# An attention kernel with a long convolution beside it: engines held to the source's order, and another order of the convolutions

## The chip, the cores and the metric

One core of a Trainium2 chip. The metric is the time of the program on the device in microseconds, the median of several runs. The engines are TensorE (PE; its weight loads are PEld), VectorE (DVE), ScalarE (ACT), GpSimd (POOL) and SyncE (SP). Here POOL and SP do hardly more than start DMAs.

## What is computed

Two independent blocks over 2048 positions; their results stand side by side in the output.

```python
# A: attention, 32 heads of 16, one shared k and v
q = (x @ wq) in 32 heads;  k = x @ wk;  v = x @ wv
p = softmax(q k^T / 4);    a = concat_heads(p v) @ wo
# B: 512 channels
k_shift = short causal convolution of k, 4 taps per channel
kv = k_shift * v
y  = long causal convolution of kv with ssm_k (2048 taps, by FFT) + kv * ssm_D
b  = q * y
```

## The kernel before

**Attention.** A *step* is one tile of 128 keys for four heads and 512 queries: `scores` (L655, PE) fills two score tiles for step i + 2, two exponentials (L663, ACT) turn them into `p`, and `pv` (L672, PE) adds `p` times v to the accumulator `acc`. There are 512 steps; 16 of them, a *group*, finish one accumulator, which VectorE copies out (`ao`, L682). The loop is `attend`. After each step it calls `fill.step(i)`.

**Fill.** `_Fill` holds five generators ("threads"). Each yields what its next piece costs in nanoseconds of PE and of DVE, or that it wants to wait some steps. At each step both accounts get a rate; a thread may go on while its accounts are positive, the first in the list first, and at most one piece with PE work per step. `RATES` lists (from step, PE rate, DVE rate); `Q_AT` lists the steps from which the four quarters of the queries are projected. The threads:

- `rest_of_q`: queries `q = x wq` (L186 with `xT,wq`), cut to two f16 parts (L525 to L530) and written to DRAM (`qd`), from where `stack` loads them (`st`, at the fifth step of a group, for the next group); and a bound (L539 to L548).
- `conv_pe`: the TensorE side of B, in two halves of 256 channels (`blk`). `long_load` and `long_forward` transform the filter `ssm_k` (`hin`; transposes L243, copies L245, products with the table `ff`, copies L193) into a spectrum `ch`. `short_load` and `short_forward` load windows of k (`kk`) and v, do the short convolution and the product with v on VectorE (L295 to L303) and transform the result `a` into a spectrum `cx`. `backward` transforms the product back (`sp,fi`) and multiplies by q (L364).
- `conv_dve`: the VectorE side: 16-point transforms (`dft16`: L124 to L137, L169 to L175) of both spectra, their product (L330), the transform back.
- `wo_heads` and `wo_part`: for each two accumulators, load the sums and the values back from DRAM (`rl`, `o`), invert the sums (L716, L717), spread them through DRAM (`rd`, `r`), scale (L724), then the products with `wo` (L186 with `wo,o`), added into `wp` (L758, L760).

Two PSUM banks have the tag `f`: one holds `acc`, the other the product of the fill, until VectorE has copied it.

**Order.** A scheduler sets the order of the instructions of ACT, DVE, POOL and SP after the source has been recorded; inside `manual_schedule(engines={PE})` PE alone keeps the order in which the source wrote its instructions. In the kernel before, that block takes in the prologue (load x, transposes, k, v, the first queries) and the attention.

Of the kernel before, what the change touches and what calls it, by code (L numbers as in the profile page):

```python
# [37 lines left out]
FT = 4  # L38
PB = 5

RATES = [(0, 440.0, 1650.0), (470, 920.0, 1650.0)]

Q_AT = 0, 50, 160, 290


def _tables():
# [29 lines left out]
WAIT = -1.0  # L76
# [3 lines left out]
class _Emit:  # L80
# [289 lines left out]
    def conv_pe(self):  # L370

        yield from self.conv_load()
        self.sp = {}
        hin = self.long_load(0)
        ch = self.spectrum()
        yield WAIT, 4
        for blk in range(D // CB):
            yield from self.long_forward(blk, hin, ch)
            self.sp["ch", blk] = ch
            self.seen.add(("ch", blk))  # L380
            tpb, kk = self.short_load(blk)
            if blk:
                yield from self.after(("y", blk - 1))
                yield from self.backward(blk - 1, *self.sp["y", blk - 1])
            cx = self.spectrum()
            yield from self.short_forward(blk, tpb, kk, cx)
            self.sp["cx", blk] = cx
            self.seen.add(("cx", blk))
            if blk == 0:
                hin = self.long_load(1)  # L390
                yield from self.after(("p", 0))
                ch = self.spectrum()
        yield from self.after(("y", 1))
        yield from self.backward(1, *self.sp["y", 1])

    def conv_dve(self):
        nat = [0, 1, 2, 3]
        for blk in range(D // CB):
            yield from self.after(("ch", blk))
            ch = self.sp["ch", blk]  # L400
            yield from self.dft16(ch, nat, nat, -1)
            yield from self.after(("cx", blk))
            cx = self.sp["cx", blk]
            yield from self.dft16(cx, nat, nat, -1)
            f1, f2 = self.places
            yield from self.product(cx, ch)
            self.seen.add(("p", blk))
            yield from self.dft16(cx, f2, f1, 1)
            self.sp["y", blk] = cx, self.places
            self.seen.add(("y", blk))  # L410
# [193 lines left out]
    def rest_of_q(self):  # L604
        for c, first in enumerate(Q_AT):
            while self.step < first:
                yield WAIT, 1
            for g in range(4):
                if c == 0 and g < 2:
                    continue  # L610
                b = None
                for dk in range(4):
                    yield (920, 0, HOLD) if dk < 3 else (920, 2600)
                    b = b or self.bank()
                    self.q_mm(g, c, b, dk)
                self.q_out(g, c, b)
                yield WAIT, 2
                yield 350, 1100
                self.bound(g, c, self.bank())
            self.seen.add(f"q{c}")  # L620
            if c < 2:
                self.xT[c + 2] = self.w.tile([P, 4, 512], F32, tag="xt", bufs=2, name=f"xT{c + 2}")
                self.nc.sync.dma_start(self.xT[c + 2], self.xd[c])
        self.flag()
# [364 lines left out]
def body(ctx, tc, I, out, parts="ab"):  # L989
    fpool = ctx.enter_context(tc.tile_pool(name="fl", bufs=1))  # L990
    ok = fpool.tile([1, 1], I32, name="ok")
    with ExitStack() as st:
        em = _Emit(st, tc, I, out)
        em.ok = ok
        st.enter_context(tc.manual_schedule(engines={mybir.EngineType.PE}))
        em.prologue()
        threads = [em.rest_of_q(), em.conv_pe(), em.wo_part(), em.wo_heads(), em.conv_dve()]
        em.attend(_Fill(threads, RATES))
    if "a" in parts:
        rv = tc.nc.values_load(ok[0:1, 0:1], min_val=0, max_val=1)  # L1000
        with tc.If(rv < 1):
            _general(tc, I, out)
# [21 lines left out]
```

## Time and profile before

| | us |
|---|---|
| median of 3 runs (1159.46 to 1162.69) | 1161.17 |
| the profiled execution | 1153.92 |
| its span, first to last instruction | 1152.1 |
| PE busy | 1059.8 |
| ACT busy | 989.6 |
| DVE busy | 633.8 |
| POOL busy | 87.8 |

The profiled execution took 1.8 us more than its span, and 0.6% less than the median of the runs. Busy time is the union of an engine's instructions; a busy PE is not PE at its peak, since ends of matmuls are modelled. The mean granted TensorE clock was 0.989. In rows of groups, the columns behind the count are the busy time, the mean length of one in ns, and the idle time just ahead of them with what ended it. Lines are those of the kernel before; in the changed kernel those of `load` (L413) and all behind it stand four lower.

### The profile page before, as it was taken

The numbers are of one execution on the slowest core, as the hardware profiler recorded it, in microseconds if no ns is written. First come the engines' busy times: TensorE is split into PE (matmuls) and PEld (weight loads), VectorE is DVE, ScalarE is ACT, GpSimd is POOL, SyncE is SP. The second block draws the span as 40 slices with busy tenths as digits, with TensorE's granted clock in tenths as the row PEclk, the third lists the DMA queues.
The fourth block names the chain that finished last, engine by engine and source line by source line (L and its number), as shares of the span: only waits on it lengthen the run. The fifth ranks groups of instructions, "written<-read, shape, count | busy, mean of one in ns | idle before, by whom it ended". The sixth has DMA issues, their size and how long they took to land.

```text
span 1152.1 us, 21936 instructions
## 1 busy us (share of the span) xinstructions
PE 1059.8 (92%) x8975; PEld 260.8 (23%) x8975; DVE 633.8 (55%) x914; ACT 989.6 (86%) x1041; POOL 87.8 (8%) x140
## 2 busy tenths in 40 slices
PE   6699999999899988999999899998999899999996
PEld 3222221221222111122222222221222111122321
DVE  3422221279976999951226932228738999711143
ACT  2399998999799878899999799999799899899882
POOL 1000000031110000000012100022110000000300
PEclk9899999999999999999999999999999999999999
DMA  8412111263241010121114211226221211121311
GB/s 283 159 33 75 59 36 54 80 187 101 67 145 57 28 45 26 56 86 34 35 59 154 81 42 34 64 92 190 95 72 54 85 43 45 44 73 29 129 33 44
DMA packets 49094, 89.55 MB, mean 78 GB/s; under 512 B 11308, under 2 KB 26202, under 8 KB 47964
## 3 DMA queue, kind: packets, MB, share of 16 engines
q1 hardware_dynamic: 36108, 46.42, 12.4%
q0 software_dynamic: 11648, 40.89, 11.1%
q8 instruction: 72, 1.18, 0.4%
q10 hardware_dynamic: 1232, 0.78, 0.2%
q14 instruction: 34, 0.28, 0.1%
HBM read 63.04 MB, written 25.02 MB: 76 GB/s over the span
## 4 chain that ended last, share of the span: by engine, by line
PE 52%; DVE 30%; ACT 6%; issue 6%; DMA 5%; SPq 0%; POOL 0%; ACTq 0%; DVEq 0%
PE f L672 24%; PE s L655 13%; PE f L186 13%; DVE sp L124 9%; ACT p L663 6%; DVE sp L330 3%; DVE a L301 2%; DVE t L299 2%; DVE t L330 1%; DMA o<-od 1%; DMA hin<-in_B_ssm_k 1%; DVE sp L175 1%; DVE u L173 1%; DVE sp L174 1%; DMA xb<-in_A_x 1%
## 5 line engine op out<-in xcount | busy, mean ns | idle before, releaser
L663 ACT ACTIVATE p<-s 128x1024 f32<-128x1024 f32 x1024 | 977.3, 1043 | 117.0 <-PE s L655 68.6
L672 PE MATMUL f<-p,vx 128*32 128x512 f32 x4096 | 548.6, 608 | 10.0 <-DVE ao L682 7.2
L655 PE MATMUL s<-st,kst 49*128 49x512 f16 x2048 | 333.7, 384 | 18.8 <-ACT p L663 9.7
L655 PEld LDWEIGHTS <-kst 49*128 49x128 f16 x2048 | 74.3, 94 | 434.3 <-issue 423.4
L672 PEld LDWEIGHTS f<-p,vx 128*32 128x32 f32 x4096 | 80.9, 108 | 199.9 <-issue 180.9
L124 DVE TENSOR_TENSOR sp<-sp 128x1024 f32<-128x1024 f32 x96 | 111.8, 1216 | 0.2
L193 DVE COPY sp<-f 128x512 f32<-128x512 f32 x64 | 44.0, 688 | 107.5 <-PE f L186 107.5
L186 PE MATMUL f<-wo,o 128*32 128x512 f32 x480 | 63.7, 602 | 10.9 <-DVE wp L760 7.2
L186 PE MATMUL f<-xT,wq 128*32 128x512 f32 x512 | 68.7, 616 | 3.7 <-DVE gm L548 2.9
L525 DVE TENSOR_SCALAR cut<-f 128x512 f32<-128x512 f32 x16 | 11.0, 689 | 97.9 <-PE f L186 97.8
L760 DVE TENSOR_TENSOR wp<-wp,f 128x512 f32<-128x512 f32 x44 | 29.9, 680 | 49.7 <-PE f L186 49.7
L124 DVE TENSOR_TENSOR sp<-sp,sp 128x1024 f32<-128x1024 f32 x48 | 56.3, 1215 | 0.0
L197 POOL DMA_DIRECT2D ff<-in_ff x32 | 17.8, 559 | 444.0 <-PE s L655 441.6
L682 DVE COPY ao<-f 128x512 f32<-128x512 f32 x31 | 21.3, 686 | 46.4 <-PE f L672 46.4
L364 DVE TENSOR_TENSOR r<-f,q 128x256 f32<-128x256 f32 x32 | 13.5, 422 | 50.8 <-PE f L186 49.2
L186 PE MATMUL f<-a,ff 128*32 128x256 f32 x512 | 33.7, 380 | 8.2 <-DVE sp L193 8.1
L186 PE MATMUL f<-sp,fi 128*32 128x256 f32 x512 | 34.5, 388 | 5.2 <-DVE r L364 5.2
L186 PE MATMUL f<-hT,ff 128*32 128x256 f32 x512 | 33.5, 379 | 0.1
L301 DVE TENSOR_TENSOR a<-a,t 128x512 f32<-128x512 f32 x48 | 32.8, 683 | 0.4
L197 POOL DMA_DIRECT2D fi<-in_fi x16 | 8.8, 553 | 311.3 <-PE s L655 311.3
L299 DVE TENSOR_TENSOR t<-kk,tpb 128x512 f32<-128x512 f32 x48 | 32.1, 683 | 0.3
L245 DVE COPY hT<-f 128x512 f32<-128x512 f32 x16 | 11.0, 688 | 38.2 <-PE f L243 38.2
(105 smaller groups left out, 543.6 us busy)
## 6 DMA issues: line engine op xcount, KB each, us to landing
ff<-in_ff POOLq DMA_DIRECT2D x32, 256.0 KB, 3.0
od<-ao SPq DMA_DIRECT2D x30, 256.0 KB
kk<-in_B_k POOLq DMA_DIRECT2D x12, 640.0 KB, 5.9
qd<-qp SPq DMA_DIRECT2D x48, 128.0 KB
st<-qd SPq DMA_DIRECT2D x60, 98.0 KB
hin<-in_B_ssm_k POOLq DMA_DIRECT2D x4, 1024.0 KB, 8.5
v<-in_B_v POOLq DMA_DIRECT2D x16, 256.0 KB, 3.6
fi<-in_fi POOLq DMA_DIRECT2D x16, 256.0 KB, 3.0
```

The source lines that it names most:

```text
L124: v.tensor_tensor(part(out), part(a), part(b), op)
L186: self.nc.tensor.matmul(out[j : j + 32], w[:, j : j + 32], x, start=start, stop=stop)
L193: self.nc.vector.tensor_copy(c[:, :, m, :], b.rearrange("p (q n) -> p q n", q=2))
L197: self.nc.gpsimd.dma_start(t, self.I[n][:, 2 * m2 : 2 * m2 + 2])
L299: nc.vector.tensor_tensor(t, kx(i), tap(i), ALU.mult)
L301: nc.vector.tensor_tensor(a, a, t, ALU.add)
L330: self.nc.vector.tensor_tensor(out, a, b, op)
L655: self.nc.tensor.matmul(s[:, e, :], self.kst[rows, k * P : (k + 1) * P], self.st[n][rows, pr, :], start=True, stop=True,)
L663: self.nc.scalar.activation(p, s, AF.Exp, scale=DH**-0.5 / SC / SC)
L672: nc.tensor.matmul(self.acc[32 * j : 32 * j + 32, :], self.vx[:, k, :], self.pt[2 * i + j // 2][:, j % 2, :], start=k == 0, stop=k == NKT - 1,
L682: nc.vector.tensor_copy(a, self.acc)
L760: nc.vector.tensor_tensor(wp, wp, b, ALU.add)
```

## The change

The block of the attention now holds all engines to the source's order, and has the attention alone; the prologue stands in a block of its own that holds PE as before. In `conv_pe` and `conv_dve` each half begins with the short convolution, then comes the filter; the list of threads has another order; `RATES` is one rate, and `Q_AT` has other steps.

```diff
-RATES = [(0, 440.0, 1650.0), (470, 920.0, 1650.0)]
-Q_AT = 0, 50, 160, 290
+RATES = [(0, 550.0, 1450.0)]
+Q_AT = 0, 60, 190, 310
...
         yield from self.conv_load()
         self.sp = {}
-        hin = self.long_load(0)
-        ch = self.spectrum()
-        yield WAIT, 4
         for blk in range(D // CB):
-            yield from self.long_forward(blk, hin, ch)
-            self.sp["ch", blk] = ch
-            self.seen.add(("ch", blk))
+            if blk:
+                yield from self.after(("p", blk - 1))
             tpb, kk = self.short_load(blk)
-            if blk:
-                yield from self.after(("y", blk - 1))
-                yield from self.backward(blk - 1, *self.sp["y", blk - 1])
             cx = self.spectrum()
             yield from self.short_forward(blk, tpb, kk, cx)
             self.sp["cx", blk] = cx
             self.seen.add(("cx", blk))
-            if blk == 0:
-                hin = self.long_load(1)
-                yield from self.after(("p", 0))
-                ch = self.spectrum()
+            hin = self.long_load(blk)
+            yield WAIT, 4
+            if blk:
+                yield from self.after(("y", blk - 1))
+                yield from self.backward(blk - 1, *self.sp["y", blk - 1])
+            ch = self.spectrum()
+            yield from self.long_forward(blk, hin, ch)
+            self.sp["ch", blk] = ch
+            self.seen.add(("ch", blk))
...
-            yield from self.after(("ch", blk))
-            ch = self.sp["ch", blk]
-            yield from self.dft16(ch, nat, nat, -1)
-            yield from self.after(("cx", blk))
-            cx = self.sp["cx", blk]
-            yield from self.dft16(cx, nat, nat, -1)
+            for n in ("cx", "ch"):
+                yield from self.after((n, blk))
+                yield from self.dft16(self.sp[n, blk], nat, nat, -1)
             f1, f2 = self.places
+            cx, ch = self.sp["cx", blk], self.sp["ch", blk]
...
-        st.enter_context(tc.manual_schedule(engines={mybir.EngineType.PE}))
-        em.prologue()
-        threads = [em.rest_of_q(), em.conv_pe(), em.wo_part(), em.wo_heads(), em.conv_dve()]
-        em.attend(_Fill(threads, RATES))
+        with tc.manual_schedule(engines={mybir.EngineType.PE}):
+            em.prologue()
+        with tc.manual_schedule():
+            threads = [em.rest_of_q(), em.wo_heads(), em.conv_pe(), em.wo_part(), em.conv_dve()]
+            em.attend(_Fill(threads, RATES))
```

The number of instructions of each kind is the same. What moves is shown at three places. The first is VectorE's queue in the prologue, around the last part of k (`kv_297`), whose largest entry (`km`, `kx`, `kmr`) is needed for `wb`. Before:

```order
L237 TENSOR_TENSOR hin_758<-hin_758,dt 128x1
L488 SCALAR_TENSOR_TENSOR kst<-kh_277,msk,kc_275 128x512
L497 COPY vx<-f_300 128x4x15
L476 TENSOR_REDUCE km<-kv_297 128x1
L498 COPY vx<-f_300 128x4
L504 TENSOR_REDUCE kx<-km 128x1
L484 TENSOR_SCALAR kc_336<-kv_297,msk 128x512
L508 COPY kmr<-f_309 128x1
L237 TENSOR_TENSOR hin_758<-hin_758,dt 128x1
L514 TENSOR_SCALAR wb<-msk,kmr 128x32
```

The same place in the changed kernel:

```order
L484 SCALAR_TENSOR_TENSOR kst<-kh_277,msk,kc_275 128x512
L493 COPY vx<-f_300 128x4x15
L472 TENSOR_REDUCE km<-kv_297 128x1
L494 COPY vx<-f_300 128x4
L500 TENSOR_REDUCE kx<-km 128x1
L480 TENSOR_SCALAR kc_336<-kv_297,msk 128x512
L504 COPY kmr<-f_309 128x1
L510 TENSOR_SCALAR wb<-msk,kmr 128x32
```

The two additions to the filter `hin`, which need its DMA, have left the prologue; nothing else moved here.

The second is VectorE's queue in the short convolution of the second half (`a` and `t` are its products and sums, `rl` and `o` belong to the heads). Before:

```order
L760 TENSOR_TENSOR wp_4929<-wp_4929,f_7500 128x512
L299 TENSOR_TENSOR t_7804<-kk_5877,tpb_5872 128x512
L716 TENSOR_SCALAR rl_9062<-rl_9062 128x32
L301 TENSOR_TENSOR a_7781<-a_7781,t_7804 128x512
L717 RECIPROCAL rl_9062<-rl_9062 128x32
L303 TENSOR_TENSOR a_7781<-a_7781,v_7777 128x512
L295 TENSOR_TENSOR a_7879<-kk_5877,tpb_5872 128x512
L299 TENSOR_TENSOR t_7881<-kk_5877,tpb_5872 128x512
L724 TENSOR_TENSOR o_7508<-o_7508,r_7509 128x512
L301 TENSOR_TENSOR a_7879<-a_7879,t_7881 128x512
```

In the changed kernel, where the short convolution of the second half meets the heads:

```order
L712 TENSOR_SCALAR rl_5071<-rl_5071 128x32
L713 RECIPROCAL rl_5071<-rl_5071 128x32
L301 TENSOR_TENSOR a_5167<-a_5167,t_5203 128x512
L303 TENSOR_TENSOR a_5167<-a_5167,v_5163 128x512
L193 COPY sp_4178<-f_5239 128x2x256
L193 COPY sp_4178<-f_5263 128x2x256
L295 TENSOR_TENSOR a_5278<-kk_4177,tpb_4172 128x512
L299 TENSOR_TENSOR t_5280<-kk_4177,tpb_4172 128x512
```

The scheduler set the operations on `rl` and `o`, which need DMAs, where it expected these; now they stand seven steps behind the DMA in the source, and the copies of a product (`L193`) right behind the last operation that the product's step has.

The third is POOL's queue from the start (after the rows that set constants). Before:

```order
L560 MEMSET vx 128x512
L197 DMA ff_821<-in_ff 128x512
L197 DMA ff_823<-in_ff 128x512
L197 DMA ff_911<-in_ff 128x512
L197 DMA ff_982<-in_ff 128x512
L227 DMA hin_758<-in_B_ssm_k 128x2048 x2
L264 DMA tpb_2355<-skd 128x256 x4
```

In the changed kernel:

```order
L556 MEMSET vx 128x512
L264 DMA tpb_548<-skd 128x256 x4
L197 DMA ff_555<-in_ff 128x512
L197 DMA ff_557<-in_ff 128x512
L280 DMA kk_553<-in_B_k 15x3x256
L280 DMA kk_553<-in_B_k 112x3x256
L281 DMA kk_553<-in_B_k 128x2x256
```

`tpb` waits for `skd`, which is written in the attention, so POOL's first table comes only then.

## The prediction

> **What bounds the kernel now.** I read the page first (shares, then the groups by line), then the busy time of each engine in stretches of the attention, then the waits and a few pieces of the timeline.
>
> ```profile
> span 1152.1 us, 21936 instructions
> ...
> PE 1059.8 (92%) x8975; PEld 260.8 (23%) x8975; DVE 633.8 (55%) x914; ACT 989.6 (86%) x1041; POOL 87.8 (8%) x140
> ...
> L663 ACT ACTIVATE p<-s 128x1024 f32<-128x1024 f32 x1024 | 977.3, 1043 | 117.0 <-PE s L655 68.6
> L672 PE MATMUL f<-p,vx 128*32 128x512 f32 x4096 | 548.6, 608 | 10.0 <-DVE ao L682 7.2
> ...
> L186 PE MATMUL f<-wo,o 128*32 128x512 f32 x480 | 63.7, 602 | 10.9 <-DVE wp L760 7.2
> L186 PE MATMUL f<-xT,wq 128*32 128x512 f32 x512 | 68.7, 616 | 3.7 <-DVE gm L548 2.9
> ...
> L186 PE MATMUL f<-sp,fi 128*32 128x256 f32 x512 | 34.5, 388 | 5.2 <-DVE r L364 5.2
> L186 PE MATMUL f<-hT,ff 128*32 128x256 f32 x512 | 33.5, 379 | 0.1
> ```
>
> TensorE and ScalarE are both near full, VectorE is at 55% of the span. The exponentials alone take 977.3 us, so a group of 16 steps (there are 32) can't take less than 977.3 / 32 = 30.5 us. The rest is work of TensorE, "fill", slipped between the steps: a product of 512 columns (8 records) costs 68.7 / 64 = 1.07 us, one of 256 columns 34.5 / 64 = 0.54. The last view on which the sum rests is this one, of single groups:
>
> ```profile
> core 0: us, PE busy (x) PEld busy (x) DVE busy (x) ACT busy (x) POOL busy (x), PEclk, DMA share, GB/s
> 116.90:148.70 31.80, 31.80 (x302) 9.29 (x300) 7.93 (x14) 30.10 (x33) 1.61 (x3) 1.00 0.19 59
> 246.10:279.30 33.20, 31.19 (x264) 6.70 (x264) 33.20 (x48) 30.40 (x33) 5.96 (x8) 1.00 0.39 125
> 279.30:317.00 37.70, 31.86 (x290) 7.89 (x288) 37.66 (x61) 31.72 (x34) 5.99 (x9) 1.00 0.27 83
> 317.00:349.70 32.70, 31.02 (x292) 7.98 (x294) 22.43 (x32) 29.37 (x32) 5.17 (x10) 1.00 0.38 131
> 349.70:384.00 34.30, 32.09 (x290) 7.57 (x288) 25.20 (x30) 32.00 (x34) 1.08 (x2) 1.00 0.19 59
> 384.00:422.70 38.70, 33.23 (x253) 6.58 (x256) 38.67 (x49) 31.02 (x33) 0.00 (x0) 0.96 0.08 24
> 494.30:525.30 31.00, 29.66 (x226) 6.28 (x224) 12.26 (x15) 29.97 (x33) 0.00 (x0) 1.00 0.23 76
> 788.50:824.80 36.30, 31.65 (x264) 7.31 (x264) 25.37 (x41) 28.96 (x31) 5.13 (x8) 0.95 0.42 133
> 858.20:891.70 33.50, 31.81 (x290) 7.79 (x288) 27.35 (x35) 31.82 (x34) 1.78 (x3) 1.00 0.18 58
> 1058.90:1097.60 38.70, 36.51 (x406) 11.27 (x405) 7.76 (x20) 32.46 (x34) 9.44 (x14) 1.00 0.36 119
> ```
>
> Where VectorE has little to do, fill sets the length. The group at 494.3 has 4.2 us of fill and takes 31.0. The one at 116.9 has 8.4 (12 products of 256 columns and three sets of transposes) and takes 31.8, with TensorE busy throughout. The one at 1058.9 has 13.6 and takes 38.7. So I use one rule: 31.2 us up to 7 us of fill, above that 24 us plus the fill (24 is 31.8 - 8.4 = 23.4 and 38.7 - 13.6 = 25.1, rounded between). Where VectorE is full the length is VectorE's: 33.20 busy of 33.2, 37.66 of 37.7, 38.67 of 38.7.
>
> ```profile
> L672 PE MATMUL f<-p,vx x4096: 592/617/1061, 51.4 to 1137.8; 128*32 128x512 f32 x196
> 1137.40 1.04 PE L672 MATMUL f<-p,vx 128*32 128x512 f32 x8
> ```
>
> The attention runs from 51.4 to 1138.4, 1087.0 us. I counted the fill that stands between two products in the program's order, group by group (groups 0 to 30 of the kernel before: 9.0, 6.0, 8.5, 7.9, 8.3, 8.6, 6.4, 6.4, 6.4, 8.5, 7.9, 8.3, 7.9, 4.3, 8.2, 8.5, 8.1, 8.5, 7.9, 8.3, 8.1, 8.5, 5.3, 8.5, 8.5, 6.4, 5.4, 4.3, 4.3, 5.4, 13.8). By the rule these give 995.0; with the last group as measured (40.9) 1035.9. **So 1087.0 - 1035.9 = 51.1 us are stalls that VectorE causes**; they are the prize. One of them:
>
> ```profile
> 796.91 0.18 DVE L716 TENSOR_SCALAR rl<-rl 128x32 f32<-128x32 f32 x1 [2.37 <-DMA rl<-od]
> 802.12 0.69 DVE L724 TENSOR_TENSOR o<-o,r 128x512 f32<-128x512 f32 x1 [2.43 <-DMA o<-od]
> 802.24 1.05 PE L186 MATMUL f<-a,ff 128*32 128x256 f32 x16
> 807.69 0.68 DVE L193 COPY sp<-f 128x512 f32<-128x512 f32 x1
> 808.43 1.07 PE L186 MATMUL f<-a,ff 128*32 128x256 f32 x16 [3.61 <-DVE sp L193]
> DVE rl L716 <- DMA rl<-od: 21.9, 8, 4.6
> DVE o L724 <- DMA o<-od: 16.2, 6, 5.6
> DVE o L724 <- DMA r<-rd: 11.1, 3, 4.5
> ```
>
> VectorE stood twice behind a DMA (2.37 and 2.43 us), came late with its other work, copied the product of 802.24 only at 807.69, and TensorE, which has one bank for fill beside the accumulator's, stood 3.61 us. The last three rows are such waits over the whole span, 49.2 us.
>
> **The change, part by part.** (1) *Prologue.* POOL no longer loads tables and `hin` during it, and the two additions to `hin` leave VectorE's queue.
>
> ```profile
> 36.08 0.16 DVE L237 TENSOR_TENSOR hin<-hin,dt 128x1 f32<-128x1 f32 x1 [2.72 <-DMA hin<-in_B_ssm_k]
> 41.18 0.16 DVE L237 TENSOR_TENSOR hin<-hin,dt 128x1 f32<-128x1 f32 x1 [2.65 <-DMA hin<-in_B_ssm_k]
> 41.75 0.61 PE L539 MATMUL f<-qa,wb 128*32 128x512 bf16 x1 [3.42 <-DVE wb L515]
> ```
>
> The second wait (2.65) stands right ahead of `wb`, for which TensorE waits; of the first I take 1.5 as passed on, through the maximum over k: 4.2 saved, at least 2.65; with the first loads of x alone on the DMA engines up to 7. `hin` now is issued at step 53 and used from step 61: 8 steps of 1.9 us, 15 us, against a landing of 8.5:
>
> ```profile
> kk<-in_B_k POOLq DMA_DIRECT2D x12, 640.0 KB, 5.9
> ...
> hin<-in_B_ssm_k POOLq DMA_DIRECT2D x4, 1024.0 KB, 8.5
> v<-in_B_v POOLq DMA_DIRECT2D x16, 256.0 KB, 3.6
> ```
>
> (2) *VectorE in the source's order.* The two DMA-fed operations of the heads now stand 7 steps (13 us) behind their DMAs, and VectorE's share of a group is at most 24.6 us, because the second rate fell from 1650 to 1450 ns a step; no group can be full of it any more. The 51.1 us go. Nothing that is hoisted comes late next: each copy stands right behind its product.
>
> (3) *POOL and SP in the source's order.* Loads are issued when the plan reaches them: `v` is issued 3 or more steps (over 5.7 us) ahead of its use with one exception at 2 steps, against 3.6 landing; the stacks of queries 10 steps ahead. At step 14 the first windows `kk` come 8 steps (15 us) after POOL began on four broadcasts and seven loads of them; one wait of some us there, ahead of no fill until step 20. I cost both at nothing beyond (5).
>
> (4) *Bunched fill.* One constant rate of 550 ns and the new starts of the queries give, group by group, 9.9, 6.4, 6.4, 10.7, 10.4, 10.4, 10.3, 10.3, 6.4, 4.3, 0, 6.4, 11.5, 8.2, 6.4, 8.5, 7.5, 9.6, 9.6, 10.7, 10.4, 10.6, 11.0, 5.4, 4.3, 5.4, 3.2, 4.3, 0, 11.7, 9.5. By the rule (30.5 where there is none) that is 1017.0 for groups 0 to 30. The last group loses the end that stood alone:
>
> ```profile
> 1129.20 1.04 PE L186 MATMUL f<-wl,lr 128*32 128x512 f32 x8
> 1131.05 1.07 PE L186 MATMUL f<-wl,lr 128*32 128x512 f32 x8 [0.81 <-DVE wp L784]
> ...
> 1135.68 1.90 PE L186 MATMUL x<-wp,ident 128*32 128x512 f32 x16
> ```
>
> From 1129.20 to 1137.40 TensorE had nothing beside these: 8.2 us. The four products now stand at steps 503 to 508 among scores, so 40.9 - 8.2 + 1.8 = 34.5. Together 1051.5, that is 15.6 more than the 1035.9 of before: fill of 10 us in one group costs what the empty groups can't give back.
>
> (5) *New stalls.* The nearest rows are the groups of before with VectorE at 22 to 27 us, not full: 317.0, 349.7, 858.2 and 788.5 lie 1.5, 1.8, 1.0 and 5.1 above the rule. The changed kernel has 22 groups with 22 to 24.6 us. The low end is 0 (a copy in its place never makes TensorE wait); the high end their mean, 2.4 x 22 = 53. Since those groups hold the DMA waits and late copies that part (2) removes, I take 0.7 x 22 = 15.
>
> Sum: -4.2 - 51.1 + 15.6 + 15 = -24.7 us. On the profiled span 1152.1 - 24.7 = 1127.4, in that execution's time (1153.9) 1129.2. The median of the runs is 1161.2, 0.6% above the profiled one; there it is **1136.5**.
>
> **Rivals.** (a) *The new stalls stay near nothing* (0 instead of 15) and the prologue gives 7: 1161.2 - 51.1 + 15.6 - 7 = 1118.7; if fill also costs 23.4 plus itself instead of 24 in the 18 groups above 7, 1108. For it: all copies in their places; against: a fill product every step or two leaves one bank, and bursts of VectorE remain (twelve operations of the last normalization at step 501).
>
> (b) *Slower: VectorE's fixed order holds TensorE.* Place: the one bank for fill, of which 204 products are copied by VectorE. A wait at VectorE's head, for a DMA or for a product that TensorE reaches late, delays every copy behind it. The `hin` rows show it: 2.65 us of waiting became 3.42 for TensorE. It decides from 24.7 + 15 = 39.7 us of new stalls, 0.19 us a copy or 1.8 a heavy group; at the full 2.4 a group the time is 1136.5 + 38 = 1174. Against it: the distances of (2) and (3). The Trainium skill, TensorE: Matmul & The Clock Gate (Architectural detail: the array is 16x 32x32), says that VectorE's queue is strictly first in, first out; the `hin` rows agree, and by it alone this rival would be the forecast.
>
> (c) *No difference:* new stalls of 36 to 43 us, 1157.7 to 1164.7. A measurement can tell about 0.3% here, 3.5 us.
>
> (d) *TensorE isn't a bound at all*: then fill is free, every group takes the exponentials' 30.5, and the attention falls to 32 x 30.5 = 976: 1161.2 - 111 - 4 = 1046. The rows at 116.9 and 494.3 speak against it: with ScalarE at 30.1 and 30.0, the one with twice the fill is longer and TensorE has no idle time. The Trainium skill, Perfetto Trace Analysis (Identifying the Most-Contended Engine), says that busy time of matmuls doesn't tell how near the limit TensorE is and that weight loads do; by their 23% this rival would hold. The trace doesn't agree where groups are compared.
>
> **How the numbers follow.** Chances: forecast 0.60 (own range 1122 to 1152, new stalls of 0.5 to 30), (a) 0.20, (b) 0.12, (c) 0.07, (d) 0.01. The range 1113 to 1156 takes in most of (a) and of the upper half of (5) (1.6 a group). Faster by over 0.3%: 0.60 + 0.20 + 0.01 = 0.81; same 0.07; slower 0.12.
>
> **What would show it.** Right: first product near 47 instead of 51.4; no group with VectorE over 26 us; no wait of L716 or L724 (now L712, L720) for a DMA; groups 3 to 7 and 19 to 22 at 34 to 35 us with TensorE full, groups 8 to 11 and 23 to 28 at 30.5 to 32. Wrong: idle time of TensorE put down to VectorE's copies above 30 us in all; `kk` or `v` waits of VectorE above 10 us; PE-full groups above 36.

## The result, and the profile after

The changed kernel takes 1115.18 us (median of 4 runs, 1114.87 to 1115.90) against 1160.32 for the kernel before in the same job (4 runs, 1154.38 to 1162.69): ratio 0.9619, 95% interval 0.9582 to 0.9656. That is 45.1 us by medians. The two profiled executions lie closer: spans of 1152.1 and 1113.6, a gain of 38.5. The kernel before happened to be profiled in an execution 6 to 7 us below its usual time. The span can be divided up, so the working below goes by it.

The page of the kernel after (shares, chain, groups by line; the chain is the work that ended last, by line):

```profile
span 1113.6 us, 21915 instructions
...
PE 1057.5 (95%) x8975; PEld 265.0 (24%) x8975; DVE 648.8 (58%) x914; ACT 991.6 (89%) x1041; POOL 87.5 (8%) x140
...
PE 73%; ACT 13%; issue 8%; DVE 4%; DMA 1%; SPq 0%; POOL 0%; ACTq 0%; DVEq 0%
...
L659 ACT ACTIVATE p<-s 128x1024 f32<-128x1024 f32 x1024 | 979.3, 1058 | 84.3 <-PE f L668 43.7
L668 PE MATMUL f<-p,vx 128*32 128x512 f32 x4096 | 548.2, 607 | 3.3 <-DVE ao L678 3.2
...
L186 PE MATMUL f<-wo,o 128*32 128x512 f32 x480 | 63.3, 600 | 2.3 <-DVE o L720 1.4
```

The engines' busy times hardly changed (TensorE 1059.8 to 1057.5 us). What shrank is the third column: idle time ahead of the accumulating products fell from 10.0 to 3.3 us, ahead of the products with `wo` from 10.9 to 2.3, ahead of the exponentials from 117.0 to 84.3. The chain that ended last runs through VectorE for 4% of the span; before it was 30%.

Busy time from the first `pv` to the last, of the kernel before and of the kernel after (columns as in the prediction):

```profile
51.40:1138.40 1087.00, 1022.26 (x8733) 243.67 (x8735) 603.19 (x842) 974.10 (x1021) 83.65 (x128) 0.99 0.22 70
```

```profile
44.10:1099.80 1055.70, 1021.18 (x8733) 247.42 (x8735) 618.25 (x844) 976.06 (x1021) 86.72 (x134) 0.99 0.23 76
```

The attention lost 31.3 us, and TensorE's idle time fell from 64.7 to 34.5, 30.2 us: the gain is TensorE waiting less. The other 7.3 us lie ahead of the first product (44.11 against 51.43). The tail after the last product kept its length.

What VectorE waits for in the kernel after (us in total, times, longest), the rows with a DMA:

```profile
DVE wq L435 <- DMA wq<-in_A_wq: 6.3, 1, 6.3
...
DVE wkv L432 <- DMA wkv<-in_A_wk: 3.0, 1, 3.0
...
DVE a L303 <- DMA v<-in_B_v: 1.6, 1, 1.6
DVE wp L754 <- DMA out<-wp: 1.1, 1, 1.1
```

The three rows of 21.9, 16.2 and 11.1 us (`rl` and `o`) are gone. Two of these four lie in the prologue, and the other two sum to 2.7 us.

Single groups of the kernel after (numbers 3, 10, 12, 22, 25 and 31):

```profile
143.20:176.94 33.74, 33.49 (x306) 8.28 (x304) 22.98 (x29) 31.37 (x34) 3.25 (x6) 1.00 0.30 108
372.60:402.00 29.40, 27.34 (x195) 5.74 (x193) 21.76 (x23) 29.40 (x33) 0.00 (x0) 1.00 0.14 45
434.50:468.48 33.98, 33.95 (x278) 7.40 (x276) 21.97 (x35) 31.13 (x33) 4.37 (x6) 1.00 0.41 133
767.00:803.30 36.30, 33.70 (x338) 9.94 (x336) 13.57 (x18) 32.41 (x34) 3.73 (x6) 0.99 0.19 63
868.70:903.30 34.60, 31.03 (x236) 6.38 (x235) 23.80 (x27) 30.81 (x34) 0.00 (x0) 1.00 0.14 46
1061.80:1099.80 38.00, 34.67 (x266) 7.31 (x268) 13.07 (x30) 27.82 (x29) 0.61 (x2) 0.91 0.05 15
```

Group 12 has 11.5 us of fill and TensorE busy for 33.95 of 33.98. Group 10 has none and takes the exponentials' time, 29.40. Two groups still hold stalls of 2.6 and 3.6 us (22 and 25), and the last one 3.3.

### The profile page after: what moved, and what is told of

Its sections match the earlier page's. It is cut to its first block, busy times and chain, and to the rows that moved or that the text cites. A ratio compares the mean times of both kernels' runs of the same rounds, so it can differ in the third digit from the quotient of the medians.

```text
span 1113.6 us, 21915 instructions
## 1 busy us (share of the span) xinstructions
PE 1057.5 (95%) x8975; PEld 265.0 (24%) x8975; DVE 648.8 (58%) x914; ACT 991.6 (89%) x1041; POOL 87.5 (8%) x140
## 4 chain that ended last, share of the span: by engine, by line
PE 73%; ACT 13%; issue 8%; DVE 4%; DMA 1%; SPq 0%; POOL 0%; ACTq 0%; DVEq 0%
PE f L668 34%; PE s L651 19%; PE f L186 17%; ACT p L659 12%; PE f L243 1%; DMA xb<-in_A_x 1%; DVE lr L787 1%; DVE sp L124 1%; DMA v<-in_B_v 1%; PE x L443 1%; PE f L458 0%; PE f L469 0%; PE f L535 0%; DVE ao L678 0%; PE x L186 0%
## 5 line engine op out<-in xcount | busy, mean ns | idle before, releaser
L659 ACT ACTIVATE p<-s 128x1024 f32<-128x1024 f32 x1024 | 979.3, 1058 | 84.3 <-PE f L668 43.7
L651 PE MATMUL s<-st,kst 49*128 49x512 f16 x2048 | 339.9, 383 | 22.6 <-ACT p L659 7.1
L193 DVE COPY sp<-f 128x512 f32<-128x512 f32 x64 | 44.2, 691 | 101.7 <-PE f L186 101.4
L186 PE MATMUL f<-xT,wq 128*32 128x512 f32 x512 | 65.8, 593 | 0.2 <-DVE gm L544 0.2
L756 DVE TENSOR_TENSOR wp<-wp,f 128x512 f32<-128x512 f32 x44 | 30.2, 687 | 57.0 <-PE f L186 56.8
L521 DVE TENSOR_SCALAR cut<-f 128x512 f32<-128x512 f32 x16 | 11.1, 691 | 80.1 <-PE f L186 80.0
L365 POOL DMA_DIRECT2D out<-r x16 | 11.4, 713 | 344.6 <-DVE r L364 338.7
L186 PE MATMUL f<-a,ff 128*32 128x256 f32 x512 | 33.5, 379 | 1.4 <-DVE sp L193 1.4
L301 DVE TENSOR_TENSOR a<-a,t 128x512 f32<-128x512 f32 x48 | 33.1, 690 | 1.6
L186 PE MATMUL f<-hT,ff 128*32 128x256 f32 x512 | 33.5, 379 | 0.0
L186 PE MATMUL f<-sp,fi 128*32 128x256 f32 x512 | 33.5, 379 | 0.0
L281 POOL DMA_DIRECT2D kk<-in_B_k x16 | 13.6, 848 | 251.5 <-DVE t L299 208.6
L299 DVE TENSOR_TENSOR t<-kk,tpb 128x512 f32<-128x512 f32 x48 | 32.8, 682 | 0.0
```

The lines of the kernel that those rows point to most:

```text
L186: self.nc.tensor.matmul(out[j : j + 32], w[:, j : j + 32], x, start=start, stop=stop)
L193: self.nc.vector.tensor_copy(c[:, :, m, :], b.rearrange("p (q n) -> p q n", q=2))
L281: nc.gpsimd.dma_start(k[:, n:5, :], self.kr[:, 2 * m2 - 3 + n : 2 * m2 + 2, cs])
L299: nc.vector.tensor_tensor(t, kx(i), tap(i), ALU.mult)
L301: nc.vector.tensor_tensor(a, a, t, ALU.add)
L651: self.nc.tensor.matmul(s[:, e, :], self.kst[rows, k * P : (k + 1) * P], self.st[n][rows, pr, :], start=True, stop=True,)
```

## The experiments

The prediction's rule gives a length for groups 0 to 30 from the fill that the plan puts into them; what is measured above it is counted as stall. It isn't all waiting: after some waits of TensorE its granted clock (`PEclk`) stands at 0.50 for 3.41 us or a multiple of it, which slows the work behind. One table for all kernels (us, each from its own trace and its own plan):

| kernel | VectorE's order | rule | measured | above | last group | median |
|---|---|---|---|---|---|---|
| before | scheduler | 995.0 | 1046.1 | +51.1 | 40.9 | 1160.3 |
| split_only | scheduler | 995.0 | 1047.2 | +52.2 | 40.9 | 1158.7 |
| plan_only | scheduler | 1017.0 | 1054.6 | +37.6 | 31.7 | 1148.3 |
| plan_split | scheduler | 1017.0 | 1055.4 | +38.4 | 31.7 | 1148.5 |
| order_only | source | 995.0 | 996.5 | +1.5 | 48.4 | 1106.7 |
| after | source | 1017.0 | 1017.7 | +0.7 | 37.9 | 1115.2 |
| near_heads | source, short waits | 1023.0 | 1051.6 | +28.6 | 33.1 | 1142.3 |
| pe_dve | source (SP, POOL: scheduler) | 1017.0 | 1015.0 | -2.0 | 35.0 | 1113.7 |
| oldrates | source | 997.0 | 996.8 | -0.2 | 43.4 | 1099.8 |
| oldconv | source | 1017.8 | 1017.0 | -0.8 | 38.0 | 1116.9 |
| dve1650 | source | 1021.0 | 1019.2 | -1.8 | 36.8 | 1116.2 |
| flat480 | source | 1004.3 | 1002.7 | -1.6 | 46.9 | 1108.0 |
| spread1 | source | 996.4 | 1002.4 | +6.0 | 44.0 | 1106.6 |
| spread2 | source | 998.9 | 1007.2 | +8.3 | 38.9 | 1106.2 |

The rule was fitted to three groups of the kernel before, so its 51.1 there was an inference. It was then met within 2 us by seven of the nine kernels in the source's order (near_heads apart), which have five plans besides the one that it was fitted to; spread1 and spread2 lie 6 and 8 us above it. It holds for the sum only: in the kernel after the groups above it exceed it by 15.6 us together, and those below fall short by 14.9. The medians come from four jobs, in which the kernel before took 1160.3, 1156.3, 1159.6 and 1159.0, so differences of 3 us between kernels of different jobs are not read.

**The two halves of the change apart.** order_only is the kernel before with these last lines changed; plan_only is the kernel after with the old ones:

```diff
-        st.enter_context(tc.manual_schedule(engines={mybir.EngineType.PE}))
-        em.prologue()
+        with tc.manual_schedule(engines={mybir.EngineType.PE}):
+            em.prologue()
+        with tc.manual_schedule():
```

> The kernel before with one edit: the prologue in a block of its own and all engines in the source's order during the attention. Rates, starts of the queries, order of the convolutions and threads as before. If the source's order carries the gain: the stalls of VectorE go and the prologue shortens by 7.3 us, 1105 to 1125 us, no group with VectorE full. If the plan (rates, order of the convolutions) carries it: only the prologue is saved, 1148 to 1156 us, and groups of 36 us and more remain.

> The changed kernel with the blocks of before: rates, starts of the queries, threads and convolutions are the new ones, but a scheduler orders ACT, DVE, POOL and SP, prologue and attention in one block. If the source's order carries the gain: 1145 to 1165 us, with waits of VectorE for DMAs of 30 us and more. If the plan carries it: 1115 to 1127 us.

order_only: 1106.68 (1106.06 to 1107.95), ratio 0.9558 [0.9516, 0.9599]. plan_only: 1148.34 (1145.12 to 1151.39), ratio 0.9925 [0.9900, 0.9949]. The source's order carries the gain: 49.6 us over the old plan (1156.26 in that job), 33.2 over the new one (1148.34 to 1115.18). The new plan alone gains 8 under the scheduler and *costs* 8.5 under the source's order (1106.68 to 1115.18). The change as made is slower than its first half.

**Is it the block or the order?** split_only puts the prologue of the kernel before into a block of its own and leaves the scheduler everything else; plan_split is the kernel after with the scheduler in the second block:

```diff
-        with tc.manual_schedule():
+        with tc.manual_schedule(engines={mybir.EngineType.PE}):
```

> The kernel before with one edit: the prologue in a block of its own; a scheduler still orders ACT, DVE, POOL and SP in both. If the loads and the two additions to hin made the prologue long: first product near 44.1 us instead of 51.4 and 1151 to 1155 us. If the shorter prologue came from the source's order: no change, 1158 to 1163 us.

> The changed kernel, but in the attention a scheduler orders ACT, DVE, POOL and SP, as before. Only the source's order is missing. If that order carries the gain of the attention: 1140 to 1160 us. If the plan carries it: 1113 to 1120 us, the attention within 5 us of 1055.7.

split_only: 1158.68, ratio 1.0006 [0.9984, 1.0028], nothing. Its first product comes at 53.37, and VectorE still waits for `hin` in the prologue (3.03 and 2.62 us); the block alone doesn't free the prologue. In order_only and in plan_split TensorE waits 0.73 us for `wb` instead of 3.42, so the order or the plan does. plan_split: 1148.47, ratio 0.9923 [0.9895, 0.9950], the same as plan_only. Two blocks do nothing by themselves. VectorE's waits for the heads' DMAs in plan_split:

```profile
DVE rl L712 <- DMA rl<-od: 26.7, 8, 6.4
DVE o L720 <- DMA r<-rd: 25.8, 7, 6.2
```

**Which engine's order?** In pe_dve, TensorE and VectorE keep the source's order and SP and GpSimd's transfers are the scheduler's again:

```diff
-        with tc.manual_schedule():
+        with tc.manual_schedule(engines={mybir.EngineType.PE, mybir.EngineType.DVE}):
```

> The kernel after, with TensorE and VectorE alone in the source's order during the attention; the scheduler places the DMAs of SyncE and GpSimd again. TensorE's, VectorE's and ScalarE's instructions stand in the same order as in after, only the two queues of transfers differ. With the scheduler on VectorE too the same plan took 1148.47. Theory A (VectorE's order carries the 33 us): 1112 to 1119. Rival B (the place of the DMA issues on SyncE or GpSimd carries part of it, by an earlier landing of o, r, kk or v): 1125 to 1148, with waits of VectorE on DMAs that after does not have.

1113.65 (1112.65 to 1117.54), ratio 0.9612 [0.9582, 0.9642]: the same as the kernel after. TensorE's and ScalarE's instructions come in the same order in this kernel, in the kernel after and in plan_split; VectorE's are those of the kernel after here and others in plan_split, which took 35 us more. So VectorE's order alone carries the 33 us. Its waits for DMAs:

```profile
DVE wq L435 <- DMA wq<-in_A_wq: 8.8, 1, 8.8
DVE r L364 <- DMA out<-r: 3.5, 1, 3.5
DVE wkv L432 <- DMA wkv<-in_A_wk: 3.0, 1, 3.0
DVE wp L754 <- DMA out<-wp: 2.3, 1, 2.3
```

Its first product comes at 47.08 instead of 44.11. Of these 3.0 us 1.7 are a lower clock (the 32 matmuls of the queries ahead of it take 5.48 instead of 3.81), so the place of the transfers, with a wait for `wq` that is 2.5 longer, is worth 1.3 at most. Its attention is 5.7 us shorter, as much as groups 23 and 31 are together. The first and second row are the kernel after (half clock, then group 23), the others groups 23 and 31 of pe_dve; group 31 of the kernel after stands above:

```profile
802.60:809.40 6.80, 6.07 (x28) 0.93 (x28) 2.40 (x4) 2.96 (x3) 0.00 (x0) 0.50 0.22 80
803.30:837.20 33.90, 32.90 (x232) 6.58 (x232) 22.56 (x30) 28.88 (x31) 0.00 (x0) 0.91 0.16 54
```

```profile
806.40:837.40 31.00, 29.98 (x232) 6.33 (x232) 22.47 (x29) 28.63 (x31) 0.00 (x0) 1.00 0.24 76
1062.10:1097.10 35.00, 31.67 (x266) 7.14 (x268) 12.99 (x30) 27.52 (x29) 0.53 (x1) 1.00 0.04 12
```

Work and idle time of TensorE are the same in both kernels (1.0 us idle in group 23, 3.3 in group 31), and so are the waits ahead, 2.6 us for `ao` and 3.1 for `wp`. The kernel after took 2.9 us longer each time, with the clock at 0.50 for 6.8 us; in pe_dve it stayed at 1.00. So the same wait is followed by a half clock in one execution and not in another.

**The waits put back.** near_heads keeps every engine in the source's order and moves two small operations of the heads up, to about one step behind their DMAs:

```diff
         nc.sync.dma_start(o, od[0])
-        yield WAIT, 7
+        yield WAIT, 1
...
         nc.sync.dma_start(r, rows.unsqueeze(1).broadcast_to([8, DH, 512]))
-        yield WAIT, 7
+        yield WAIT, 1
```

> The kernel after with both waits of heads() shortened from 7 steps to 1: the reciprocal of l and the product o*r now stand in VectorE's fixed order about one step (2 us) behind the DMA that they need, where they stood seven steps (15 us) behind. Nothing else is changed but the places that follow from it. Theory A (the gain came from removing VectorE's waits for those DMAs, because a waiting VectorE holds up the copies that free TensorE's banks): the trace shows waits of rl and o on DMAs of 2 to 5 us each, 50 to 120 us in all over 30 places, and the time goes back up to 1140 to 1190. Rival B (what gains is that each engine has a fixed order at all, those waits were beside the path): the waits appear and the time stays within 1110 to 1122. Rival C (the DMAs land within a step, nothing changes): no waits of rl or o in the list, 1113 to 1118.

1142.25 (1140.89 to 1146.68), ratio 0.9857 [0.9829, 0.9885]: 27 us of the 45 are given back for three small operations at 15 places, as theory A had it. Its waits, and one of them in the timelines of VectorE and of TensorE:

```profile
DVE o L720 <- DMA r<-rd: 64.3, 15, 8.8
...
DVE rl L712 <- DMA rl<-od: 13.7, 6, 4.9
```

```profile
533.96 0.69 DVE L720 TENSOR_TENSOR o<-o,r 128x512 f32<-128x512 f32 x1 [8.84 <-DMA r<-rd]
534.57 0.68 DVE L303 TENSOR_TENSOR a<-a,v 128x512 f32<-128x512 f32 x1
535.17 0.68 DVE L193 COPY sp<-f 128x512 f32<-128x512 f32 x1
```

```profile
527.31 1.05 PE L186 MATMUL f<-a,ff 128*32 128x256 f32 x16
...
530.36 1.06 PE L668 MATMUL f<-p,vx 128*32 128x512 f32 x8
535.91 1.94 PE L186 MATMUL f<-a,ff 128*32 128x256 f32 x16 [4.49 <-DVE sp L193]
```

VectorE stands 8.84 us for `r`; behind that stand the copy of 535.17 and, behind the copy, TensorE for 4.49 us. The copy's product, that of 527.31, had been done for some 7 us. The waits sum to 78.0 us, and the groups lie 28.6 above the rule. Not all of that is waiting. Groups 0 to 30 are 33.9 us longer than in the kernel after (6.0 by the rule, since the fill moves too); TensorE's idle time in them is 21.9 longer. The clock stood at 0.50 for 30.7 us against 6.8, in seven stretches, six of them behind an idle time of 2.0 to 4.5 us: the product of 535.91 takes 1.94 us, that of 527.31 took 1.05. At half speed for 23.9 us more, TensorE loses up to 12.0, an estimate. So a fixed order loses too, without a scheduler, when it puts a DMA's wait at VectorE's head. What such waits cost in the kernel before is another question; it is taken up below. The Trainium skill, TensorE: Matmul & The Clock Gate (Architectural detail: the array is 16x 32x32), has VectorE's queue strictly first in, first out; this timeline agrees: the copy, whose product was long there, waited for a DMA that it doesn't need.

**Which part of the new plan costs 8.5 us?** Against the kernel after, oldrates takes the rates of before; oldconv takes the order of the convolutions of before (long first); dve1650 changes VectorE's rate alone; flat480 both rates:

```diff
-RATES = [(0, 550.0, 1450.0)]
+RATES = [(0, 440.0, 1650.0), (470, 920.0, 1650.0)]   # oldrates
+RATES = [(0, 550.0, 1650.0)]                         # dve1650
+RATES = [(0, 480.0, 1650.0)]                         # flat480
```

> The kernel after with the rates of before, (0, 440, 1650) and (470, 920, 1650), in place of (0, 550, 1450); the order of the convolutions, the starts of the q projections and the threads stay as after has them. From the run with before's plan in the source's order (1106.68) and after (1115.2), the new plan costs 8.5 us. Theory A (the rates cost it: 550 a step fills groups with 10 to 11 us and leaves others with 0 to 4): 1105 to 1110, and no group of 16 steps below 30 us with no fill at all. Rival B (the order of the convolutions, or the thread order, costs it): 1113 to 1117.

> The kernel after with the order of the convolutions of before (long first for the first half, transforms of ch before cx); rates, starts and thread order stay as after has them. Theory A (the rates cost the 8.5 us, the order of the convolutions nothing): 1112 to 1117. Rival B (the order of the convolutions costs them): 1105 to 1109.

> The kernel after with rates (0, 550, 1650): the planner may give a step more VectorE work, TensorE's 550 stays. The rates of before took 15 us off after (1099.8 against 1115.2). Theory A (TensorE's rate of 550 costs them, since fill on consecutive steps cannot be made up): 1111 to 1119. Rival B (VectorE's rate of 1450 costs them, since it delays the convolution): 1098 to 1106.

> The kernel after with the rates (0, 480, 1650) for the whole attention: less TensorE fill in a step than 550, more than before's 440, so that the end is not left with 34 us of fill as in the run with before's plan in the source's order (its last two groups took 36.8 and 48.4 us). Theory A (the length of a group of 16 steps is about the larger of 23 us plus its fill and 29.4 plus 0.4 of it, so an even spread is shortest): the last group 42 to 46 us, groups of 8 to 10 us fill at 31.5 to 33.5, the time 1101 to 1107, faster than after and no slower than before's plan in the source's order. Rival B (groups with 26 us of VectorE work are held by it, as in the run with the scheduler): these groups take over 34 us and the time is over 1110.

oldrates: 1099.83 (1097.35 to 1100.45), ratio 0.9479 [0.9463, 0.9495]; below its expected 1105, so the rates cost 15.4 us and not 8.5, and what else is new in the plan gains some 7 beside order_only (5.0 of it in the last group, where order_only has one idle time of 4.73 us against 3.09 and works at half clock for 10.2 us against 3.4; so how much of it is the plan stays open). oldconv: 1116.90, ratio 0.9635 [0.9619, 0.9651]: the order of the convolutions does nothing by itself. dve1650: 1116.17, ratio 0.9623 [0.9599, 0.9647]: VectorE's 1450 does nothing either, so TensorE's 550 is what costs. flat480: 1108.00, ratio 0.9552 [0.9536, 0.9568], a miss by 1 us: groups 0 to 30 came 1.6 below the rule, the last took 46.9, with 13.7 us at half clock (the profiled execution was the slowest of four, 3.8 us above the median). Groups 5 and 12 of oldrates, with 7.7 and 8.0 us of fill, and its last:

```profile
207.20:238.20 31.00, 30.97 (x251) 6.63 (x249) 5.66 (x11) 29.71 (x33) 0.00 (x0) 1.00 0.09 29
430.60:462.30 31.70, 31.36 (x252) 6.76 (x250) 26.56 (x34) 30.20 (x32) 0.00 (x0) 1.00 0.22 67
...
1041.30:1084.70 43.40, 39.49 (x346) 9.70 (x348) 16.80 (x37) 28.33 (x28) 2.47 (x4) 0.96 0.08 25
```

VectorE is busy for 26.56 us in the second and for 5.66 in the first, and the lengths differ by 0.7: in the source's order a VectorE load of 26.56 us doesn't set the length, though it lies above the 24.6 that the prediction thought needful.

**An emptier end.** spread1 and spread2 look for a plan that leaves less to the last two groups (80 us in oldrates):

```diff
-RATES = [(0, 550.0, 1450.0)]
+RATES = [(0, 450.0, 1700.0), (416, 500.0, 1750.0)]   # spread1
+RATES = [(0, 440.0, 1750.0), (352, 540.0, 1650.0)]   # spread2, threads in before's order
-Q_AT = 0, 60, 190, 310
+Q_AT = 0, 60, 170, 300
```

> The kernel after with rates (0, 450, 1700) and (416, 500, 1750) and the third and fourth q projection at steps 170 and 300. A steady fill of about one product of four matmuls every second step, and no remainder of convolution in the last two groups: counted from the plan, the last two groups get 10 and 20 us of fill where the rates of before leave 14 and 19 to 25. Theory A (what is left of the loss sits in the last two groups, 80 us in the run with the rates of before where two groups of 32 would be 64): the last two groups 73 to 75, the time 1092 to 1098. Rival B (1700 a step fills VectorE to 27 to 29 us in a group of 31.5, and its copies come late): groups of over 33 us where VectorE has over 27, the time 1100 to 1110.

> The kernel after with rates (0, 440, 1750) and (352, 540, 1650), the q projections at 0, 60, 170, 300 and the thread order of before. Theory A (steady fill and an emptier end): the last group 38 to 42 us, the time 1091 to 1098. Rival B (VectorE at 28 to 29 us in a group holds TensorE; 540 a step from step 352 bunches the fill again): 1100 to 1110.

Both missed: 1106.64 (ratio 0.9555 [0.9522, 0.9588]) and 1106.20 (0.9542 [0.9513, 0.9570]). The ends came nearly as planned (76.3 and 71.2 us for the last two groups), but groups 0 to 30 came 6.0 and 8.3 us above the rule. The times are those of rival B; its mechanism isn't shown. TensorE's idle time in these groups is 27.2 and 27.5 us against 25.3 in oldrates, 2 us more, and the clock stood at half for 3.4 and 10.2 us against none, worth up to 1.7 and 5.1; the rest stays open. Of the five groups of spread1 with VectorE over 27 us, one takes over 33. Groups 10 and 25 of spread1:

```profile
365.70:399.90 34.20, 32.30 (x260) 6.79 (x258) 26.21 (x29) 30.69 (x33) 0.00 (x0) 1.00 0.13 39
853.10:886.60 33.50, 30.80 (x237) 6.28 (x235) 27.15 (x29) 30.64 (x34) 0.00 (x0) 1.00 0.18 51
```

TensorE is idle 1.9 and 2.7 us in them with VectorE at 26 to 27. Whether it is VectorE's load or the place of single copies isn't settled: group 12 of oldrates has the same load and no stall. The best version that was run is oldrates, 1099.83, 15 us below the kernel after.

## Why the prediction was right or wrong

The direction was right, and so was the place of the gain: VectorE's order. The measured time lies inside the range, but outside the forecast's own part of it (1122 to 1152), next to rival (a)'s 1118.7. By steps, in us of the profiled span:

| term | predicted | measured |
|---|---|---|
| prologue | -4.2 | -7.3 |
| VectorE's stalls removed | -51.1 | -51.1 by the rule |
| bunched fill, groups 0 to 30 | +22.0 | +21.2 to +22.0 |
| last group | -6.4 | -3.0 |
| new stalls | +15 | +0.7 |
| sum | -24.7 | -38.5 |

The second row is the rule's own figure on both sides; between runs, order_only against before, it is 49.6. The tail behind the attention makes up the last 0.2.

**New stalls: the step that failed.** The prediction took 0.7 us for each of 22 groups from groups of the kernel before "not full" of VectorE's work. The prediction itself said that those hold the very waits being removed, and still charged for them. Groups 0 to 30 measured 1017.7 against the rule's 1017.0, order_only 996.5 against 995.0. In the place of 15 stands about 1 (in pe_dve, with the same order of VectorE, -2.0; group 23 at half clock is the difference). TensorE's waits for VectorE in the kernel after:

```profile
PE f L668 <- DVE ao L678: 3.2, 3, 2.6
PE f L186 <- DVE wp L780: 3.1, 1, 3.1
...
PE f L186 <- DVE o L720: 1.4, 1, 1.4
PE f L186 <- DVE sp L193: 1.4, 1, 1.4
```

**The stalls removed** were right in size: the same plan with and without the scheduler, order_only against before, differs by 49.6 us in groups 0 to 30. Not all of it was waiting: TensorE's idle time in these groups fell by 39.2 us, the time at half clock from 17.1 to 5.1 us. That VectorE's order is the cause is shown by pe_dve. Part (2) named two ways in which it acts. The first, a DMA at VectorE's head ahead of a copy, is real, as near_heads shows, but it isn't the larger one in the kernel before. The second is a VectorE full of its own work: in nine groups (6, 7, 10 to 12, 17, 25 to 27) it is busy for 94 to 100% of the time, as in three of the prediction's rows. These lie 38 us above the rule, of the 51.1 in all, and hold 1.0 us of the 49.2 of waits for `rl` and `o`. The groups that hold 47.4 us of these waits lie some 8 above it, 5 of that in group 22, from which the prediction's example came; group 30 has 8.2 us of them and lies 0.8 above. In order_only the fullest group has VectorE busy for 28.1 of 32.8 us. The scheduler had put more of VectorE's work into the same groups: 227 us in groups 6 to 12, where order_only has 174. No run takes the full groups apart from the waits, so the split is read from groups and not shown by experiment.

**Bunched fill** was right: 1017.7 - 996.5 = 21.2 measured between the two plans, and the rates as its cause are shown by oldrates and dve1650. The groups named came less far apart than predicted: 3 to 7 at 32.9 to 33.7 instead of 34 to 35, 19 to 22 at 33.5 to 36.3, and the empty ones at 29.4 instead of 30.5. The rule is too steep at both ends; its errors cancel. Of the groups called at 30.5 to 32, three were longer (11, 23 and 25; 23 at half clock, 25 with its stall). Of the other signs, VectorE's load stayed under 26 us in each group and `v` was waited for 1.6 us; one group, 22, passed the 36 us that would have spoken against the steps, with 2.6 us of idle time in it.

**The last group** took 37.9, not 34.5. The burst of VectorE operations that rival (a) named at step 501 is there: `wp` L780 above is one wait of 3.1 us. But pe_dve has the same wait, and its last group takes 35.0, near the forecast; what it lacks is the half clock behind the wait. So 2.9 of the 3.4 us are the clock, for which the prediction had no term. Under the scheduler the new plan's last group took 31.7, the old one's 40.9; in the source's order 37.9 and 48.4. There the scheduler was the better one: in plan_split VectorE computes the reciprocals of the last normalization in steps 496 to 498, in the kernel after in steps 502 to 504, and TensorE's idle time in the group is 0.2 us instead of 3.3.

**The prologue** gave more than its upper bound of 7. `wb` is waited for 0.73 us instead of 3.42 and `kx` 1.24 instead of 2.79, 4.2 together, as the step had it; the third part it didn't have. TensorE's granted clock (column before the last two), ahead of and in the first queries of the kernel before, then its 32 matmuls, then both of the kernel after:

```profile
38.00:41.70 3.70, 0.33 (x2) 0.24 (x2) 0.94 (x6) 0.00 (x0) 0.00 (x0) 0.52 0.77 258
41.70:48.00 6.30, 6.25 (x41) 2.70 (x41) 3.11 (x7) 0.00 (x0) 0.00 (x0) 0.74 0.03 5
```

```profile
41.76 5.40 PE L186 MATMUL f<-xT,wq 128*32 128x512 f32 x32
```

```profile
36.00:40.00 4.00, 3.99 (x35) 1.91 (x36) 2.44 (x5) 0.00 (x0) 0.00 (x0) 1.00 0.02 1
```

```profile
36.01 0.39 PE L535 MATMUL f<-qa,wb 128*32 128x512 bf16 x1 [0.73 <-DVE wb L511]
36.02 3.81 PE L186 MATMUL f<-xT,wq 128*32 128x512 f32 x32
```

The 0.52 and 0.74 are means of windows: the clock was at 0.50 from 38.2 to 45.0 us and at 1.00 on both sides. It fell behind the wait of 2.79 us for `kx`, before the 3.42 us for `wb` began, and the matmuls behind both took 1.6 us more. The Trainium skill, TensorE: Matmul & The Clock Gate (Part 1: The HAM clock gate), puts the fall behind at least one idle window of about 3.4 us; here it came behind 2.79 us. It isn't tied to these waits either: in oldrates, with the prologue of the kernel after and its waits of 1.24 and 0.73 us, the same 32 matmuls took 5.51 us. So 1.6 of the 7.3 us are the luck of the executions profiled. The last 1.5 lie ahead of `wb` and stay unexplained; whether they are the loads of x, on which the prediction's bound of 7 rests, isn't shown. The size of the gain isn't sure to a microsecond: kernels with this same prologue begin their first product between 42.9 and 46.5.

**From span to median.** The forecast took terms read from an execution of 1153.9 us off a median of 1161.2. The kernel after was profiled at 1115.4, at its median. Of the miss of 21.3 us, 13.8 belong to the terms and the rest to that step. The distance goes with the clock: in 20 executions of the kernel before in one later job, the seven under 1156 us had mean granted clocks of 0.983 to 0.988, the five above 1160 us 0.980 to 0.982.

**The rivals.** (a) was the nearest: new stalls near nothing and about 7 from the prologue. (b), a fixed order of VectorE that holds TensorE, is real: near_heads shows it with 28.6 us above the rule, below the 39.7 from which the change would have lost. What kept it away is the distance of seven steps. (d), TensorE no bound, fell: in the source's order, too, a group with 11.5 us of fill takes 33.98 with TensorE idle for 0.03, one without 29.40.

## What to carry to other kernels

An operation fed by a DMA that stands too early in an in-order engine's queue costs whatever waits behind it; look at the list of that engine's waits for DMAs, and ask what stands behind each: the sum of the waits isn't their cost. Look as well for stretches in which the engine is full, however low its mean: VectorE was busy for 55% of the span, and nine full groups held 38 of the 51 us. When groups of equal work differ in length, fit the undisturbed ones and call the rest stalls; but don't carry the disturbed groups' surplus over to a version that removes the disturbance. Test the parts of a change apart: here the order alone gained 50 us, and a table of rates shipped with it took 15 back.

## What was not expected of the hardware

A wait of TensorE can be paid twice. Behind idle times mostly of 2.0 to 4.7 us its granted clock stood at 0.50, for 3.41 to 13.7 us: in the prologue before, the 32 matmuls took 5.40 us instead of 3.81, and near_heads worked at half clock for 30.7 us of its groups 0 to 30. The length of the idle time doesn't decide it alone: 2.63 us were followed by it in the kernel after, 2.62 us at the same place of pe_dve weren't. And VectorE at 26.6 us of 31.7 in a group left TensorE all but undisturbed (oldrates, group 12: 31.36 of 31.70 busy), while 8.84 us of waiting at its head cost TensorE 4.49 at once.
